# A 2-D Fourier transform ahead of a PReLU network: rows turned by ScalarE and GpSimd, and values split ahead of a butterfly

## The chip, the cores and the metric

One core of a Trainium2 chip. The metric is the device time of one execution in microseconds. TensorE multiplies into PSUM, VectorE, ScalarE and GpSimd do the rest; each of the five engines works through its own instructions in order and waits for the others by semaphores.

## The reference, cut to what matters

```
def _attn_ref(x):                       # x: 8 x 3072 x 256, float32
    X = np.fft.fft(x, axis=1)
    X = np.fft.fft(X, axis=2)
    return X.real.astype(np.float32)

def _moe_ref(x, w_in, w_out, alpha):    # x: 24576 x 256; 256 x 2048, 2048 x 256, 2048
    h = x @ w_in
    g = np.maximum(h, 0.0) + alpha * np.minimum(h, 0.0)
    return g @ w_out
```

The second takes the first's result, with its batches and rows put one behind the other.

## The kernel before, in words

**The steps.** The output is made in 26 blocks of columns, up to 512 wide. The eight batches b have three blocks each, the first and the last four. A block has 16 steps, one for each 128 of the 2048 hidden units, so there are 416 steps s = 16 g + f. The code calls a step's place within its batch the round r.

One step of TensorE holds six matmuls of `ffn1` for step s + 3 (`LEAD` = 3: two groups of three, each group into one PSUM bank of the pool `pq`, lines L665 to L667) and twelve of `ffn2` for step s (into four accumulator banks, L748; in the first block's steps up to f = 13 eight at L732). At the end of a block the accumulators are copied out, two by ScalarE (L762) and two by VectorE (L764), and stored.

**What lies between the two.** `pair(s + 3)` follows on the other engines. `sums` (VectorE, L683) makes `pf` from the first bank and the row `xbc`. Then for each half i of 0 and 1: `row` makes `d` = `pf` minus or plus the second bank (VectorE, L691) and `ad`, which is `d` times a scale, on ScalarE (L695), into the half's own PSUM bank. `split` takes `d` and `ad` of the step before: VectorE makes their maximum, which is the PReLU (L647; L644 for steps below `WHOLE` = 14), ScalarE rounds it to `hi` (L649), and GpSimd makes the rest `lo` = `d` - `hi` (L651). `st1` holds the values that have `d` and `ad` but aren't split yet, `st2` those that `ffn2` may use. With the read of `ad` in `split` the half's bank is free.

**The four banks.** The pool `pq` has four banks, handed out in the order of the program among those that have no more readers to come. The transforms of the next batch use the same banks. So `other_bank`, which `dft` calls for a bank, first splits the first half (i = 0) of whatever is under way.

**The transform.** While a batch is in its steps, the next one is folded along its rows by GpSimd and VectorE (`fold_piece`, up to round 36, in the first batch 50), into the tiles `ce`, `co`, `se` and `so` of 128x6x128. The scratch tiles of the fold have the tags `xev` and `xeg`, one buffer each. Then the even tiles go through `unit` (four times), and the odd ones through `turn_rows` and `mids` (rounds 44 and 46; 60 and 62 in the first batch) and, in rounds 0 and 3 of their own batch, `unit_odd`. The first batch has its own `turn_rows` in rounds 12 and 13, without `mids`, the second of them right behind `fold_128` (two small copies on GpSimd), and its `unit_odd` in rounds 16 and 19.

`turn_rows` takes the six planes of 128x128 of an odd tile in pairs: planes 3 to 5 times a tangent for each partition, plus planes 0 to 2, into the tile `a` (names `aco`, `aso`), and planes 0 to 2 times the negative tangent, plus planes 3 to 5, in place (`fco`, `fso`). These are six instructions of VectorE (L443). `mids` rounds the middle plane of both to `mh` (ScalarE, L479) and makes the rest `ml` (GpSimd, L480).

`unit_odd` issues the products `ca` and `sb` of the two (L501, L504), each into one bank, and then a butterfly of each: ScalarE copies half of the bank to `os` (L512), VectorE adds and subtracts it (`y`, L523, two instructions). VectorE puts the two results together (`yo`, L545, L547, in tiles with the tags `xev` and `xeg`), and `to_x` writes them as high and low part (ScalarE L575, GpSimd L576) to `X`, which `ffn1` reads.

The order of each engine's instructions is that of the program (`manual_schedule`); the round numbers place the work by hand:

```
            if q in (0, 3):
                unit_odd(b, ("co", "so")[q // 3])
...
                for nm, at in zip(("se", "ce", "co", "so"), (51, 52, 60, 62) if b == 0 else (37, 37, 44, 46)):
                    if r == at:
                        if nm[1] == "o":
                            turn_rows(b + 1, nm)
                        mids(b + 1, nm)
```

Of the kernel before, what the change touches and what calls it, by code (L numbers as in the profile page):

```python
# [9 lines left out]
F32 = mybir.dt.float32  # L10
# [6 lines left out]
ACTF = mybir.ActivationFunctionType  # L17
ALU = mybir.AluOpType

NB, N, D, DFF = 8, 3072, 256, 2048  # L20
P = 128
# [3 lines left out]
WM = 512  # L25
# [23 lines left out]
def _place(b, kind):  # L49

    return {"ee": 0, "eo": 385, "o": 769}[kind[1:]] + (b == 0 and kind[1:] != "ee")
# [82 lines left out]
def fft2_prelu_ffn(ctx: ExitStack, tc: tile.TileContext, t, outputs):  # L134
# [6 lines left out]
    foldp = ctx.enter_context(tc.tile_pool(name="foldp", bufs=1))  # L141
    small = ctx.enter_context(tc.tile_pool(name="small", bufs=1))
    work = ctx.enter_context(tc.tile_pool(name="work", bufs=2))
# [8 lines left out]
    V, S, G = nc.vector, nc.scalar, nc.gpsimd  # L152
# [3 lines left out]
    alpha, turns = consts[:, 0:KF], consts[:, KF:KF + 6]  # L156
    sg = small.tile([P, KF], F32, name="sg")
# [80 lines left out]
    def other_bank():  # L238

        for s, i in list(st1):  # L240
            if i == 0 and s >= WHOLE:
                split(s, i)
        return pq.tile([P, 512], F32, tag="pq", name="ps")
# [7 lines left out]
    WHOLE, KEPT = 14, 8  # L251
# [133 lines left out]
    def fold_sums(i):  # L385

        b, c, h = PIECES[i]
        r = buf["x", i].rearrange("p (j i) s d -> p i s j d", i=2)
        ps = accp.tile([P, 512], F32, tag=f"acc{(i + 1) // 2}", name="fold")
        for k in range(2):  # L390
            for n, (i_, s_) in enumerate(((0, 0), (0, 1), (1, 0), (1, 1))):
                nc.tensor.matmul(
                    out=ps[:, 256 * k:256 * k + 256], lhsT=ident[:, k * (i_ ^ s_)], rhs=r[:, i_, s_],
                    start=(n == 0), stop=(n == 3),
                )
        use("x", i)
        halves = ps.rearrange("p (k a j d) -> p k j a d", k=2, a=2, j=2)
        v = foldp.tile([P, 2, 2, 64], F32, tag="xeg", name="xeg")
        S.activation(out=v, in_=halves[:, :, 1], func=ACTF.Copy)
        return halves[:, :, 0], v  # L400
# [37 lines left out]
    def turn_rows(b, nm):  # L438

        v, a = fold[b, nm], fold[b, "a" + nm]  # L440
        for out, i, j in ((a, 1, 0), (v[:, 3:6], 0, 1)):
            for c in range(3):
                V.scalar_tensor_tensor(  # L443
                    out=out[:, c], in0=v[:, 3 * i + c], scalar=turns[:, 3 * j + c:3 * j + c + 1],
                    in1=v[:, 3 * j + c], op0=ALU.mult, op1=ALU.add,
                )

    def rows_384():

# [37 lines left out]
    def dft(kind, v, zr, m, mid=None, bank=None):  # L487

        ps = (bank or other_bank())[0:m]
        tab, at = TABS[kind]  # L490
        n = tab.shape[-1]
        even, odd = [(v[:, 0], tab[:, at])], [(v[:, 2], tab[:, at + 3])]
        if zr is not None:
            even.append((zr, tab[:, 4]))
        if mid is None:
            even.append((v[:, 1], tab[:, at + 1]))
            odd.append((v[:, 1], tab[:, at + 2]))
        else:
            (fh, fl), (th, tl) = mid, middle[kind]
            for i, (lhsT, rhs) in enumerate(((fh, th), (fh, tl), (fl, th))):  # L500
                nc.tensor.matmul(out=_pairs(ps[:, 0:2 * n]), lhsT=lhsT, rhs=_halves(rhs), start=(i == 0), stop=False)  # L501
        for o, terms in ((0, even), (n, odd)):
            for i, (lhsT, rhs) in enumerate(terms):
                nc.tensor.matmul(  # L504
                    out=ps[:, o:o + n], lhsT=lhsT, rhs=rhs, start=(mid is None and i == 0),
                    stop=(i == len(terms) - 1 and (o > 0 or mid is None)),
                )
        return ps, n, m

    def odd_sums(ps, n, m):  # L510
        os = foldp.tile([P, 193], F32, tag="os", name="os", bufs=2)[0:m, 0:n]
        S.activation(out=os, in_=ps[:, n:2 * n], func=ACTF.Copy)  # L512
        return ps, os, n, m

    def butterfly(ps, n, m, last=None):
        return both_sums(*odd_sums(ps, n, m), last=last)

    def both_sums(ps, os, n, m, pool=foldp, tag="y", last=None):
        wide, bufs = (WM, 1) if tag == "pf" else (WX, 2)
        last = last or n  # L520
        y = pool.tile([P, wide], F32, tag=tag, name="y", bufs=bufs)[0:m, 0:n + last]
        for i, (op, k) in enumerate(((ALU.subtract, n), (ALU.add, last)) if n == 193 else ((ALU.add, n), (ALU.subtract, n))):
            V.tensor_tensor(out=y[:, i * n:i * n + k], in0=ps[:, 0:k], in1=os[:, 0:k], op=op)  # L523
        return y
# [9 lines left out]
    def mid_of(nm, i):  # L534
        return [m[:, i * P:(i + 1) * P] for m in middle[nm]] if nm in middle else None

    def unit_odd(b, nm, whole=True):

        z = zres[:, 1 if nm == "co" else 2]
        ps = [  # L540
            dft("ca", fold[b, "a" + nm], z, P, mid_of(nm, 0)), dft("sb", fold[b, nm][:, 3:6], None, P, mid_of(nm, 1)),
        ]
        ya, yb = (butterfly(*v, last=192) for v in ps)
        y = [foldp.tile([P, 512], F32, tag="xe" + e, name="yo")[:, 0:385] for e in "vg"]
        V.tensor_tensor(out=y[0], in0=ya, in1=yb, op=ALU.add)  # L545
        for o, n, at in ((0, 192, 1), (192, 191, 194)):
            V.tensor_tensor(out=y[1][:, o:o + n], in0=ya[:, at:at + n], in1=yb[:, at:at + n], op=ALU.subtract)  # L547
        at = _place(b, nm)
        for o, v in ((0, y[0]), (385, y[1][:, 0:383])):
            if nm == "so":  # L550
                nc.sync.dma_start(out=xcd[b:b + 1, at + o:at + o + v.shape[-1]], in_=v[0:1])
            to_x(0 if nm == "co" else 2, at + o, v, G)

    def unit(b, kind, lo_engine):
        sums = unit_mm(b, kind, pq.tile([P, 512], F32, tag="pq", name="ps"))
        for s, i in list(st1):
            if i == 0:
                split(s, i)
        unit_store(b, kind, lo_engine, butterfly(*sums))
# [13 lines left out]
    def to_x(s, c, v, lo_engine):  # L573
        hi, lo = (X[:, s + i, X0 + c:X0 + c + v.shape[-1]] for i in range(2))
        S.activation(out=hi, in_=v, func=ACTF.Copy)  # L575
        lo_engine.tensor_tensor(out=lo, in0=v, in1=hi.bitcast(F32), op=ALU.subtract)  # L576
# [58 lines left out]

    st1, st2 = {}, {}

    def split(s, i):

        d, ad, f = st1.pop((s, i))  # L640
        w = d.shape[-1]
        if s < WHOLE:
            g = work.tile([P, WM], F32, tag=f"hi{i}", name="gw", bufs=3)[:, 0:w]
            V.scalar_tensor_tensor(out=g, in0=d, scalar=sg[:, f:f + 1], in1=ad, op0=ALU.mult, op1=ALU.max)  # L644
            st2[s, i] = g
            return
        V.scalar_tensor_tensor(out=d, in0=d, scalar=sg[:, f:f + 1], in1=ad, op0=ALU.mult, op1=ALU.max)  # L647
        hi = work.tile([P, WM], F32R, tag=f"hi{i}", name="hi", bufs=3)[:, 0:w]
        S.activation(out=hi, in_=d, func=ACTF.Copy)  # L649
        lo = work.tile([P, WM], F32R, tag=f"lo{i}", name="lo", bufs=3)[:, 0:w]  # L650
        G.tensor_tensor(out=lo, in0=d, in1=hi.bitcast(F32), op=ALU.subtract)  # L651
        st2[s, i] = hi, lo

    psum = {}

# [158 lines left out]
    sums = {0: fold_sums(0)}  # L814
# [67 lines left out]
    for b in range(NB):  # L882
# [3 lines left out]
        for r in range(len(mine) * KF):  # L886
            s = mine[0] * KF + r
            g, f = divmod(s, KF)
            step(s)
            if b == 0:  # L890
                if r == 3:
                    G.memset(X[:, :, X0 + SINGLE:X0 + SINGLE + 7].bitcast(F32), 0.0)  # L892
                    nc.sync.dma_start(out=er, in_=t["er"])
                if r == 9:
                    column_128_store("ceo", butterfly(*column_128_mm("ceo")))
                if r in (10, 11):
                    unit(0, ("ceo", "seo")[r - 10], G)
                if r in (12, 13):
                    if r == 13:
                        fold_128(0)  # L900
                    turn_rows(0, ("co", "so")[r - 12])
                if r == 25:
                    start.close()
                    late = ctx.enter_context(tc.tile_pool(name="late", bufs=1))
                if r in TABLE_STEPS:
                    parts_table(list(TABS)[TABLE_STEPS.index(r)])
# [3 lines left out]
            if q in (0, 3):  # L910
                unit_odd(b, ("co", "so")[q // 3])
# [85 lines left out]
```

## Time and profile before

| what | value |
| --- | --- |
| median of 3 runs | 1694.53 us (1693.9 to 1694.86) |
| profiled execution | 1695.3 us |
| its span, first to last instruction | 1693.5 us |
| mean granted clock of TensorE | 0.996 |
| TensorE busy | 1647.7 us, 97% |
| VectorE busy | 1533.3 us, 91% |
| GpSimd busy | 1295.1 us, 76% |
| ScalarE busy | 1112.9 us, 66% |

All times that are read from the trace count from the start of the span. In the rows PE is TensorE, PEld its loading of weights, DVE VectorE, ACT ScalarE, POOL GpSimd and SP the engine that issues most transfers. L443 is line 443 of the kernel. A matmul's end is modelled and reaches into the next one, so TensorE's pace is read from starts. A group of instructions says what it writes and reads by the names of the program's tiles (out<-in).

### The profile page before, as it was taken

To read this page: it belongs to the slowest core of one execution; us is meant where nothing else is said; L and a number is where in the kernel's file an instruction comes from. 1 tells how busy PE (TensorE), PEld (TensorE's weight loads), DVE (VectorE), ACT (ScalarE), POOL (GpSimd) and SP (SyncE) were. 2 spreads that over 40 slices of the span, in tenths; PEclk is the share of its full clock that TensorE was granted. 3 is DMA by queue.
4 is the path that set the end of the run, shared out by engine and by line. 5 is a ranking of instruction groups with operands and counts; after the bars stand their busy time and mean duration, and the time that the engine had idled before them with its cause. 6 is when DMAs were issued, how large, how long until landed. Compare 5 with 4: busy or idle time off the path is not lost.

```text
span 1693.5 us, 26291 instructions
## 1 busy us (share of the span) xinstructions
PE 1647.7 (97%) x8154; PEld 1460.6 (86%) x8154; DVE 1533.3 (91%) x2726; ACT 1112.9 (66%) x1998; POOL 1295.1 (76%) x1388
## 2 busy tenths in 40 slices
PE   8999999999999999999999999999999999999998
PEld 6678898888878888788888888888887888889998
DVE  7889999899899998999989998899989999899997
ACT  5856776666666666666666666666666666667675
POOL 2358996788868887689876998678886888766666
PEclk9999999999999999999999999999999999999999
DMA  6310110010100110001100011001010010000000
GB/s 236 130 62 6 57 68 20 7 62 22 55 26 14 62 38 32 26 19 57 63 7 32 38 45 57 25 8 64 26 50 26 19 45 31 1 31 24 25 20 20
DMA packets 25290, 69.94 MB, mean 41 GB/s; under 512 B 6174, under 2 KB 7486, under 8 KB 25150
## 3 DMA queue, kind: packets, MB, share of 16 engines
q1 hardware_dynamic: 24398, 67.80, 11.3%
q8 instruction: 65, 1.06, 0.3%
q14 instruction: 75, 0.61, 0.1%
q10 hardware_dynamic: 752, 0.45, 0.1%
HBM read 42.98 MB, written 25.25 MB: 40 GB/s over the span
## 4 chain that ended last, share of the span: by engine, by line
PE 82%; DVE 11%; issue 2%; POOL 2%; ACT 1%; DMA 1%; DVEq 0%; ACTq 0%; SPq 0%; POOLq 0%
PE acc L748 50%; PE pq L665 9%; PE pq L667 8%; PE pq L666 8%; DVE d L691 3%; PE ps L504 3%; DVE d L647 2%; DVE pf L683 2%; PE ps L501 1%; PE acc L732 1%; POOL lo L651 1%; DVE aco L443 1%; DVE aso L443 1%; ACT hi L649 1%; DVE fso L443 0%
## 5 line engine op out<-in xcount | busy, mean ns | idle before, releaser
L651 POOL TENSOR_TENSOR lo<-d,hi 128x512 fp32r<-128x512 f32 (+2 forms) x804 | 974.6, 1227 | 268.9 <-ACT hi L649 251.4
L649 ACT ACTIVATE hi<-d 128x512 fp32r<-128x512 f32 (+2 forms) x804 | 483.3, 601 | 394.0 <-DVE d L647 307.3
L647 DVE SCALAR_TENSOR_TENSOR d<-d,sg,pq 128x512 f32<-128x512 f32 (+2 forms) x804 | 563.8, 701 | 0.2 <-ACT pq L695 0.2
L695 ACT ACTIVATE pq<-d,sga 128x512 f32<-128x512 f32 (+2 forms) x804 | 527.3, 656 | 48.9 <-DVE d L691 47.5
L691 DVE TENSOR_TENSOR d<-pf,pq 128x512 f32<-128x512 f32 (+2 forms) x832 | 530.6, 639 | 12.4 <-POOL lo L651 4.1
L748 PE MATMUL acc<-hi,woh 128*128 128x512 f32 (+2 forms) x1608 | 455.2, 365 | 0.0
L748 PE MATMUL acc<-hi,wol 128*128 128x512 f32 (+2 forms) x1608 | 394.2, 365 | 0.0
L748 PE MATMUL acc<-lo,woh 128*128 128x512 f32 (+2 forms) x1608 | 393.0, 364 | 0.0
L683 DVE SCALAR_TENSOR_TENSOR pf<-xbc,w,pq 128x512 f32<-128x512 f32 (+2 forms) x416 | 297.8, 716 | 71.9 <-PE pq L667 65.0
L665 PE MATMUL pq<-X,wih 128*128 128x512 f32 (+2 forms) x832 | 317.2, 381 | 31.6 <-DVE d L647 28.0
L748 PEld LDWEIGHTS acc<-hi,woh 128*128 128x128 f32 x1608 | 298.5, 189 | 31.0
L748 PEld LDWEIGHTS acc<-hi,wol 128*128 128x128 f32 x1608 | 295.9, 189 | 32.1 <-DVE o L764 0.3
L748 PEld LDWEIGHTS acc<-lo,woh 128*128 128x128 f32 x1608 | 295.4, 189 | 30.9
L666 PE MATMUL pq<-X,wih 128*128 128x512 f32 (+2 forms) x832 | 302.4, 364 | 2.7 <-POOL X L892 2.5
L667 PE MATMUL pq<-X,wil 128*128 128x512 f32 (+2 forms) x832 | 302.5, 364 | 0.0
L665 PEld LDWEIGHTS pq<-X,wih 128*128 128x128 f32 x832 | 157.3, 189 | 71.6 <-DVE d L647 25.1
L666 PEld LDWEIGHTS pq<-X,wih 128*128 128x128 f32 x832 | 157.6, 189 | 16.5 <-POOL X L892 2.8
L667 PEld LDWEIGHTS pq<-X,wil 128*128 128x128 f32 x832 | 157.5, 189 | 15.6 <-DVE wil L337 0.2
L523 DVE TENSOR_TENSOR y<-ps,os 128x193 f32<-128x193 f32 (+3 forms) x132 | 40.5, 353 | 54.2 <-ACT os L512 54.1
L383 POOL TENSOR_TENSOR raw<-raw 128x512 f32<-128x512 f32 (+2 forms) x84 | 69.3, 825 | 0.0
L289 POOL TENSOR_TENSOR w<-we,wm 128x512 int32<-128x512 int32 x16 | 20.3, 1270 | 52.3 <-DVE wm L280 47.9
L576 POOL TENSOR_TENSOR X<-yo,X 128x385 fp32r<-128x385 f32 (+1 forms) x32 | 29.1, 932 | 28.6 <-ACT X L575 28.6
(155 smaller groups left out, 1027.2 us busy)
## 6 DMA issues: line engine op xcount, KB each, us to landing
raw<-in_xh SPq DMA_DIRECT2D x46, 512.0 KB
out<-o SPq DMA_DIRECT2D x36, 512.0 KB
raw<-in_w SPq DMA_DIRECT2D x15, 512.0 KB
xbc<-xcd SPq DMA_DIRECT2D x18, 256.0 KB
out<-o SPq DMA_DIRECT2D x10, 386.0 KB
out<-o SPq DMA_DIRECT2D x6, 384.0 KB
before<-in_xh SPq DMA_DIRECT2D x2, 512.0 KB
xbc<-xcd SPq DMA_DIRECT2D x5, 193.0 KB
```

The source lines that it names most:

```text
L383: yield size, lambda o=o, i0=i0, i1=i1, op=op: e.tensor_tensor(out=o, in0=i0, in1=i1, op=op)
L504: nc.tensor.matmul(out=ps[:, o:o + n], lhsT=lhsT, rhs=rhs, start=(mid is None and i == 0), stop=(i == len(terms) - 1 and (o > 0 or mid is ...
L647: V.scalar_tensor_tensor(out=d, in0=d, scalar=sg[:, f:f + 1], in1=ad, op0=ALU.mult, op1=ALU.max)
L649: S.activation(out=hi, in_=d, func=ACTF.Copy)
L651: G.tensor_tensor(out=lo, in0=d, in1=hi.bitcast(F32), op=ALU.subtract)
L665: nc.tensor.matmul(out=out, lhsT=wih[:, f, q], rhs=xh, start=True, stop=False)
L666: nc.tensor.matmul(out=out, lhsT=wih[:, f, q], rhs=xl, start=False, stop=False)
L667: nc.tensor.matmul(out=out, lhsT=wil[:, f, q], rhs=xh, start=False, stop=True)
L683: V.scalar_tensor_tensor(out=_pairs(pf), in0=_halves(xbc[g]), scalar=w128[:, f:f + 1], in1=_pairs(ps[0]), op0=ALU.mult, op1=ALU.add,)
L691: V.tensor_tensor(out=d, in0=pf, in1=ps[1], op=ALU.add if i else ALU.subtract)
L695: S.activation(out=ad, in_=d, func=ACTF.Copy, scale=sga[:, f:f + 1])
L748: nc.tensor.matmul(out=out, lhsT=wt[:, f, o * P:(o + 1) * P], rhs=rhs, start=(f == 0 and n[o] == 0), stop=(f == KF - 1 and n[o] == 2),)
```

## The change

`turn_rows` no longer uses VectorE: for each of the two results ScalarE multiplies three planes by their tangents into a scratch tile (tag `xev` for the first, `xeg` for the second), and GpSimd adds three planes in one instruction. All six multiplications are issued ahead of the two additions. `split` is cut into `split_sum` (VectorE's maximum) and `split_parts` (`hi` and `lo`). `unit_odd` calls `split_sum` for all values under way as soon as both products are issued, which leaves the second half, since `other_bank` has split the first; then ScalarE's copies `os` of both products are issued, then `split_parts`, then the additions of both butterflies. Elsewhere `split` does what it did.

```
     def turn_rows(b, nm):
 
         v, a = fold[b, nm], fold[b, "a" + nm]
-        for out, i, j in ((a, 1, 0), (v[:, 3:6], 0, 1)):
+        made = []
+        for e, i in (("v", 1), ("g", 0)):
+            part = foldp.tile([P, 512], F32, tag="xe" + e, name="part")[:, 0:384].rearrange("p (c d) -> p c d", c=3)
             for c in range(3):
-                V.scalar_tensor_tensor(
-                    out=out[:, c], in0=v[:, 3 * i + c], scalar=turns[:, 3 * j + c:3 * j + c + 1],
-                    in1=v[:, 3 * j + c], op0=ALU.mult, op1=ALU.add,
-                )
+                at = 3 * (1 - i) + c
+                S.activation(out=part[:, c], in_=v[:, 3 * i + c], func=ACTF.Copy, scale=turns[:, at:at + 1])
+            made.append(part)
+        G.tensor_tensor(out=a, in0=v[:, 0:3], in1=made[0], op=ALU.add)
+        G.tensor_tensor(out=v[:, 3:6], in0=v[:, 3:6], in1=made[1], op=ALU.add)
...
-        ya, yb = (butterfly(*v, last=192) for v in ps)
+        parted = [(s, i, *split_sum(s, i)) for s, i in list(st1)]
+        sums = [odd_sums(*v) for v in ps]
+        for v in parted:
+            split_parts(*v)
+        ya, yb = (both_sums(*v, last=192) for v in sums)
...
-    def split(s, i):
+    def split_sum(s, i):
 
         d, ad, f = st1.pop((s, i))
+        g = d
+        if s < WHOLE:
+            g = work.tile([P, WM], F32, tag=f"hi{i}", name="gw", bufs=3)[:, 0:d.shape[-1]]
+            st2[s, i] = g
+        V.scalar_tensor_tensor(out=g, in0=d, scalar=sg[:, f:f + 1], in1=ad, op0=ALU.mult, op1=ALU.max)
+        return (g,)
+
+    def split_parts(s, i, d):
         w = d.shape[-1]
...
+    def split(s, i):
+        g = split_sum(s, i)
+        if s >= WHOLE:
+            split_parts(s, i, *g)
```

## Rows read from the trace of the kernel before

**Rows 1.** The page: busy time, share of the span, instructions of each engine.

```profile
PE 1647.7 (97%) x8154; PEld 1460.6 (86%) x8154; DVE 1533.3 (91%) x2726; ACT 1112.9 (66%) x1998; POOL 1295.1 (76%) x1388
```

**Rows 2.** Busy time by stretch: from:to, length, engines, granted clock, DMA.

```profile
100.00:150.00 50.00, 43.79 (x235) 38.42 (x234) 42.14 (x90) 29.64 (x65) 34.24 (x41) 1.00 0.06 21
...
276.00:300.00 24.00, 19.98 (x94) 16.96 (x94) 21.56 (x41) 14.40 (x28) 14.73 (x15) 0.93 0.09 34
300.00:478.00 178.00, 178.00 (x836) 156.16 (x835) 163.39 (x269) 116.87 (x196) 147.58 (x153) 1.00 0.10 35
478.00:504.00 26.00, 23.24 (x107) 19.11 (x106) 24.73 (x46) 15.41 (x30) 16.69 (x17) 1.00 0.10 41
...
678.00:704.00 26.00, 23.24 (x108) 19.08 (x107) 24.75 (x45) 16.32 (x31) 16.53 (x16) 1.00 0.10 41
1480.00:1530.00 50.00, 47.58 (x265) 43.89 (x264) 45.90 (x93) 32.12 (x65) 31.89 (x34) 1.00 0.07 26
```

**Rows 3.** The chain that ended last, 470 to 506 us: start, length, what.

```profile
474.94 0.76 DVE pf L683
...
486.50 0.66 DVE d L647
...
493.46 0.45 PE pq L665
```

**Rows 4.** Timeline, 474 to 497 us: start, length, engine; in brackets idle before, releaser.

```profile
474.08 0.38 PE L665 MATMUL pq<-X,wih 128*128 128x512 f32 x1
...
477.18 2.57 POOL L651 TENSOR_TENSOR lo<-d,hi 128x512 fp32r<-128x512 f32 x2 [1.50 <-ACT hi L649]
...
477.97 0.38 PE L665 MATMUL pq<-X,wih 128*128 128x512 f32 x1
...
478.12 2.04 DVE L443 SCALAR_TENSOR_TENSOR aco<-fco,consts 128x128 f32<-128x128 f32 x3
...
478.30 0.69 ACT L695 ACTIVATE pq<-d,sga 128x512 f32<-128x512 f32 x1
...
481.12 0.75 DVE L683 SCALAR_TENSOR_TENSOR pf<-xbc,w,pq 128x512 f32<-128x512 f32 x1
...
482.58 0.48 PE L665 MATMUL pq<-X,wih 128*128 128x512 f32 x1 [0.56 <-DVE d L647]
...
496.78 0.33 PE L501 MATMUL ps<-mh 128*128 128x386 f32 x1
```

**Rows 5.** Timeline behind the products of the third batch's first odd transform.

```profile
499.60 0.54 ACT L512 ACTIVATE os<-ps 128x193 f32<-128x193 f32 x2
...
499.95 1.15 DVE L523 TENSOR_TENSOR y<-ps,os 128x193 f32<-128x193 f32 x4 [1.00 <-ACT os L512]
...
500.72 0.45 PE L665 MATMUL pq<-X,wih 128*128 128x512 f32 x1 [0.51 <-DVE y L523]
```

**Rows 6.** Groups by line: count | busy us, mean ns | idle before, releaser.

```profile
L443 DVE SCALAR_TENSOR_TENSOR aco<-fco,consts 128x128 f32<-128x128 f32 x24 | 15.9, 713 | 0.0
...
L545 DVE TENSOR_TENSOR yo<-y 128x385 f32<-128x385 f32 x16 | 9.0, 564 | 0.6
...
L479 ACT ACTIVATE mh<-aco 128x128 fp32r<-128x128 f32 x7 | 2.2, 312 | 6.5 <-DVE aco L443 6.5
...
L576 POOL TENSOR_TENSOR X<-y,X 128x384 fp32r<-128x384 f32 x16 | 15.8, 988 | 4.4 <-ACT X L575 3.6
```

**Rows 7.** Line L651: duration in ns, least/median/most, first and last start.

```profile
L651 POOL TENSOR_TENSOR lo<-d,hi x804: 990/1281/1743, 105.2 to 1685.6; 128x512 fp32r<-128x512 f32 x116, 128x386 fp32r<-128x386 f32 x26, 128x384 fp32r<-128x384 f32 x19
```

**Rows 8.** Timeline of the first two batches: three waits.

```profile
114.60 0.88 DVE L443 SCALAR_TENSOR_TENSOR aso<-fso,consts 128x128 f32<-128x128 f32 x3 [1.43 <-POOL fso L420]
...
131.32 0.40 PE L665 MATMUL pq<-X,wih 128*128 128x384 f32 x1 [0.70 <-DVE d L647]
...
290.12 0.48 PE L665 MATMUL pq<-X,wih 128*128 128x512 f32 x1 [1.96 <-DVE d L647]
```

More of the change, by code (lines that the diff above doesn't have):

```diff
@@ L636, in fft2_prelu_ffn @@
     st1, st2 = {}, {}
-    def split(s, i):
+    def split_sum(s, i):
         d, ad, f = st1.pop((s, i))
-        w = d.shape[-1]
[L642 to L647, printed above, removed]
+        g = d
[5 more added lines that the diff above has]
+    def split_parts(s, i, d):
+        w = d.shape[-1]
         hi = work.tile([P, WM], F32R, tag=f"hi{i}", name="hi", bufs=3)[:, 0:w]
```

## The prediction, made before the result was known

> **What bounds the kernel now.** I read the page first: TensorE is busy 97% of the span, VectorE 91%, GpSimd 76%, ScalarE 66% [rows 1]. So the question is not which engine is fullest, but where TensorE stands still and for whom. The table by stretches answers the first half. From 300 to 478 us, one whole stretch between two batches, TensorE is busy 178.00 of 178 us: nothing can be won there. In the 26 us around a change of batch it is busy 23.24; the rows of the second and third such change are the same to 0.01 us, and there are five of this kind. The first batch (100 to 150 us), the step to the second (276 to 300 us) and the step to the last (1480 to 1530 us) lack 6.2, 4.0 and 2.4 us [rows 2]. The chain of work that ended last says for whom: from 474.94 to 493.46 us not one matmul is on it, only VectorE with short stretches of issue [rows 3]. The change of batch is bound by VectorE, all else by TensorE.
>
> The timeline shows how [rows 4]. A step of 18 matmuls takes 477.97 - 474.08 = 3.89 us. Then `turn_rows` puts six instructions on VectorE: it starts them at 478.12, and the next step's `pf` follows at 481.12 instead of 474.94 + 3.89 = 478.83. The PSUM banks of `ffn1` come free with VectorE's `split` (the line L647), so the next step's first matmul starts at 482.58, 4.61 us after the one before. From 477.97 to the first product of `unit_odd` at 496.78 there are four steps, 18.81 us where 4 x 3.89 = 15.56 would do: 3.25 us lost for the two turns of a batch. The idle times that the rows name understate this: the gap of 0.56 us cost 4.61 - 3.89 = 0.72 us, and the second matmul behind a gap starts about 0.1 us late as well. I count 0.26 us on top of each gap.
>
> **What the turns cost after the change.** The change takes 6 x 16 = 96 instructions from VectorE (the costliest quarter of them means 713 ns [rows 6]) and adds 6 x 16 multiplications on ScalarE and 2 x 16 additions of 128x384 on GpSimd. For ScalarE the nearest row is the 128x128 `mh`, 312 ns; for GpSimd the 128x384 subtraction of `to_x`, 988 ns [rows 6]. No row shows these very operations. From below, the six could overlap at their ends and take less than 6 x 0.31; from above, a GpSimd pass could cost what the dearest `lo` did, 1743 ns [rows 7], which I keep for the range.
>
> In total that is some 30 us of ScalarE and 32 us of GpSimd, both with room. What matters is the queue. Behind the turn ScalarE has `mids`, which since the change waits for GpSimd's sums; ScalarE works in order, so the `hi` and `ad` of the next step are held too, and VectorE's `split` waits for `ad`. Take the first turn in numbers of [rows 4, 6]. ScalarE is done with `ad` at 478.30 + 0.69 = 478.99. Three multiplications: 479.93; six: 480.86. GpSimd has finished both `lo` at 477.18 + 2.57 = 479.75, so its sums run 479.93 to 480.92 and on to 481.91. The second `mh` ends at 482.22, then one `hi` and one `ad` of at most 0.69 us each: 483.60. Without a delay VectorE comes to the `split` that needs this `ad` one `pf` after 474.94 + 2 x 3.89 = 482.72, at 482.72 + 0.75 = 483.47. ScalarE is 0.13 us late, and the bank that this `split` frees is needed only by the matmuls at 477.97 + 2 x 3.89 = 485.75, so TensorE doesn't see it. But no slack is left: whatever the sums take beyond this goes through.
>
> The second turn is followed by the copies of the finished accumulators on ScalarE, held by the same wait; the matmul that needs the second of them then comes about 0.1 us too early. After that TensorE has the products of `unit_odd`, in which ScalarE catches up. I leave 0.15 us of the 3.25.
>
> GpSimd's other work is not late by this: `lo` of the held step is needed two steps later, and the fold of the next batch has ended before (round 36, the turns are at 44 and 46). The two buffers that the products take are those of the fold and of `yo`, both done with by then. No DMA is added, and no queue's order changes but that of the row that `unit_odd` sends, which waits for the same `yo`.
>
> **What the split made early brings.** In `unit_odd` only the first half of the values under way is split today; the second half's `split` stands behind the butterflies and the next `pf`. The second `ffn1` group then takes a bank of the products and waits 0.51 us for the butterfly [rows 5]; with 0.26 on top that is 0.77 us. After the change the second half's `split` stands ahead of the butterflies. Its `ad` comes before `os` on ScalarE, and VectorE idles 1.00 us there for `os` [rows 5], more than one `split` takes (0.66 us [rows 3]). It costs nothing, and the wait goes. In the first batch the same pattern costs more: 0.70 us at 131.32 [rows 8], the first of three such gaps.
>
> **A rule against it.** GpSimd needs 988 ns for 384 columns where VectorE's `yo` of 385 columns, also from SBUF, needs 564: 1.75 times as much [rows 6]. The Trainium skill ("GPSIMD Engine Reference", section 4.1, Engine selection) says to add tiles on VectorE, as GpSimd is about twice as slow with two inputs; the trace agrees in direction. By its factor a sum would take an estimated 1.13 us, the hold at each of 14 turns would be 0.28 us longer, and the result 3.9 us later, near 1665 us; the sum below keeps to the row.
>
> **The sum.** Five ordinary changes of batch: 3.25 + 0.77 - 0.15 = 3.87 us each, 19.3 us.
> The second batch: gaps of 4.0 us [rows 2] at four places, 1.0 on top, and a granted clock of 0.93 over 24 us, 1.7 us: the clock sinks behind the gap of 1.96 us [rows 8]. 6.7 us in all. Its steps are narrower on TensorE while VectorE's are not, so I leave 0.9 us: 5.8 won.
> The last batch: 2.4 us of gaps [rows 2] at six places, 1.6 on top, and by the starts of its matmuls 0.5 at short stalls without a gap: 4.5, of which I leave 0.8: 3.7.
> The first batch: 5.6 us of the 6.2 [rows 2] (0.6 belong to a `unit`, which isn't changed), at eight places, 1.9 on top: 7.5. Its second turn waits today for GpSimd's copy `fold_128`, 1.43 us [rows 8]; after the change ScalarE waits for that same copy, with its own queue behind it. I leave 2.1: 5.4 won.
> Together 19.3 + 5.8 + 3.7 + 5.4 = 34.2 us. The profiled execution took 1695.3 us, so 1661.1; the median of the runs is 0.8 us below it. I predict 1661 us. If nothing is left over, 20.1 + 6.7 + 4.5 + 7.5 = 38.8 us go: 1656.5.
>
> **Rivals.**
> *ScalarE becomes the new wait.* For it speaks that the working above ends without slack. If a sum takes 1743 ns, the second `mh` ends 2 x 0.755 = 1.5 us later, and at 14 turns (those of the first batch have no `mids`) that is 21 us: 1682; half of it: 1672. Against it: no 128x384 row of GpSimd here is near that price. Chance 0.15.
> *The early split doesn't free the bank in time.* Then 5 x 0.77, some 2.5 in the first batch and 1.2 in the last are not won, 7.6 us: 1669. Against it is VectorE's idle time ahead of the butterflies. Chance 0.07.
> *Nothing is won.* The hold on ScalarE just replaces that on VectorE. It needs 34.2 / 14 = 2.4 us more per turn, sums of 2.2 us each: 1692 to 1698. Chance 0.05.
> *Slower.* The same place, GpSimd's two sums ahead of `mids`, past that point: at 2.6 us each the hold grows by 2 x 1.61 = 3.2 us, 45 us in all against 34 won: 1706. VectorE's first product of a turn does take several times as long as its last beside GpSimd (its three need 2.04 us at 478.12 [rows 4]), so such prices exist; but with the turn gone, what VectorE does meanwhile (`pf`, `d`, `split`) reads one input from PSUM, as it does beside every `lo`. Chance 0.03.
> The forecast has what is left, 0.70, with a range of its own of 1656 to 1668.
>
> **The numbers.** A measurement of this kernel tells 0.2% (3.4 us) from no change. The three cases ahead of "nothing is won" are all faster: 0.70 + 0.15 + 0.07 = 0.92; the same 0.05; slower 0.03. The range that leaves out no more than 2 in 10 goes from 1655 (all stalls gone, by the median) to 1677, which takes in the early split's failure and the milder two thirds of ScalarE's.
>
> **What would show it.** Right: around 478 to 504 us VectorE has no work of a turn, TensorE's waits for `split` there are gone, the clock stays at 1.00 near 290 us, and ScalarE's `mh` waits for GpSimd about 1 us. The bank step: no wait for `y` behind `unit_odd`. Wrong: GpSimd's sums above 1.2 us each, VectorE idle ahead of `split` for `ad`, or a wait of TensorE for ScalarE's copies of the accumulators at the end of a batch.

## The result, and the profile after

The changed kernel takes 1675.0 us (median; 1674.0 to 1675.8) against 1694.2 of the kernel before: a ratio of 0.9887, interval 0.987 to 0.9904, 19.2 us faster. That lies in the range, but the predicted time was 1661, with 34 us won: the change brought little more than half of it. (The result and the experiments are medians of several executions; a profile is of one of them, up to 3 us longer or shorter.)

The page of the changed kernel, its line of busy times and the chain's shares by engine:

```profile
PE 1642.9 (98%) x8154; PEld 1462.0 (87%) x8154; DVE 1512.8 (90%) x2630; ACT 1133.8 (68%) x2094; POOL 1328.4 (79%) x1420
...
PE 88%; DVE 6%; POOL 2%; issue 2%; ACT 1%; DVEq 0%; POOLq 0%; ACTq 0%
```

Against [rows 1] VectorE has its 96 instructions less and 20.5 us less work, where [rows 6] put the costliest quarter of them alone at 15.9 us; so some of its work has become longer. The table by stretches (as in [rows 2]; the changes of batch now come earlier):

```profile
270.00:304.00 34.00, 32.15 (x162) 27.92 (x161) 30.92 (x51) 25.36 (x55) 26.37 (x26) 1.00 0.06 24
304.00:472.00 168.00, 167.80 (x789) 147.42 (x788) 155.02 (x252) 110.62 (x187) 142.41 (x148) 1.00 0.10 37
472.00:500.50 28.50, 27.78 (x131) 23.75 (x130) 25.51 (x40) 21.88 (x47) 23.33 (x23) 1.00 0.10 38
```

Between the batches TensorE is as busy as before. Around an ordinary change of batch it now stands still for 28.50 - 27.78 = 0.72 us, where the same 28.5 us of the kernel before (478 to 506.5) had 2.76. Near 290 us the clock stays at 1.00.

The timeline of the changed kernel around the first turn of the third batch, which answers to [rows 4]:

```profile
472.29 0.69 ACT L709 ACTIVATE pq<-d,sga 128x512 f32<-128x512 f32 x1
...
472.92 1.85 ACT L446 ACTIVATE part<-fco,consts 128x128 f32<-128x128 f32 x6
...
473.97 1.01 POOL L448 TENSOR_TENSOR aco<-fco,part 128x384 f32<-128x384 f32 x1 [0.26 <-ACT part L446]
...
474.94 1.00 POOL L449 TENSOR_TENSOR fco<-fco,part 128x384 f32<-128x384 f32 x1
...
475.97 0.31 ACT L482 ACTIVATE mh<-fco 128x128 fp32r<-128x128 f32 x1 [0.65 <-POOL fco L449]
...
476.71 0.67 ACT L709 ACTIVATE pq<-d,sga 128x512 f32<-128x512 f32 x1
...
477.41 0.75 DVE L652 SCALAR_TENSOR_TENSOR d<-d,sg,pq 128x512 f32<-128x512 f32 x1
```

The turn went as worked out: the six multiplications take 1.85 us, each sum 1.0, the second `mh` ends 3.30 us after the last `ad` of the step before (predicted 3.23), and the held `ad` ends at 477.38, 0.03 us ahead of the `split` that needs it. TensorE doesn't wait.

Behind `unit_odd` it does. First the kernel before, for comparison (timeline, 497 to 503 us), then the changed kernel's timeline that answers to [rows 5]:

```profile
497.26 3.79 POOL L651 TENSOR_TENSOR lo<-d,hi 128x512 fp32r<-128x512 f32 x3 [1.86 <-ACT hi L649]
...
501.13 0.56 DVE L545 TENSOR_TENSOR yo<-y 128x385 f32<-128x385 f32 x1
501.61 0.62 DVE L547 TENSOR_TENSOR yo<-y 128x192 f32<-128x192 f32 x2
```

```profile
485.83 7.79 POOL L660 TENSOR_TENSOR lo<-d,hi 128x512 fp32r<-128x512 f32 x6 [1.03 <-ACT hi L658]
...
489.91 0.75 DVE L652 SCALAR_TENSOR_TENSOR d<-d,sg,pq 128x512 f32<-128x512 f32 x1 [0.16 <-ACT pq L709]
...
490.73 1.16 DVE L526 TENSOR_TENSOR y<-ps,os 128x193 f32<-128x193 f32 x4
...
491.92 0.57 DVE L552 TENSOR_TENSOR yo<-y 128x385 f32<-128x385 f32 x1
...
492.41 2.51 DVE L554 TENSOR_TENSOR yo<-y 128x192 f32<-128x192 f32 x2
...
493.59 1.12 POOL L583 TENSOR_TENSOR X<-yo,X 128x385 fp32r<-128x385 f32 x1
...
494.84 0.75 DVE L697 SCALAR_TENSOR_TENSOR pf<-xbc,w,pq 128x512 f32<-128x512 f32 x1
...
498.60 0.48 PE L679 MATMUL pq<-X,wih 128*128 128x512 f32 x1 [0.28 <-DVE d L652]
...
499.94 0.45 PE L679 MATMUL pq<-X,wih 128*128 128x512 f32 x1 [0.43 <-DVE d L652]
```

The early `split` at 489.91 does lie in VectorE's idle time, and the wait for `y` is gone. But the two short `yo` instructions take 2.51 us; in the kernel before they took 0.62, behind GpSimd's last `lo`, which had ended at 501.05. Now they start while GpSimd is still in its row of six `lo`, which ends at 493.62, and then in `to_x`. VectorE comes to the next `pf` late, and two steps on TensorE waits for `split` twice, about 1.2 us by the starts of its matmuls, where 0.77 was to go.

### The profile page after: what moved, and what is told of

Read it like the earlier page. It is cut to its first block, busy times and chain, and to the rows that moved or that the text cites. A ratio compares the mean times of both kernels' runs of the same rounds, so it can differ in the third digit from the quotient of the medians.

```text
span 1673.9 us, 26326 instructions
## 1 busy us (share of the span) xinstructions
PE 1642.9 (98%) x8154; PEld 1462.0 (87%) x8154; DVE 1512.8 (90%) x2630; ACT 1133.8 (68%) x2094; POOL 1328.4 (79%) x1420
## 4 chain that ended last, share of the span: by engine, by line
PE 88%; DVE 6%; POOL 2%; issue 2%; ACT 1%; DVEq 0%; POOLq 0%; ACTq 0%
PE acc L762 54%; PE pq L679 9%; PE pq L680 9%; PE pq L681 9%; PE ps L507 3%; DVE d L705 2%; PE ps L504 2%; PE acc L746 1%; DVE pf L697 1%; DVE d L652 1%; POOL lo L660 1%; PE fold L392 0%; PE ps L320 0%; DVE we L276 0%; DVE wm L280 0%
## 5 line engine op out<-in xcount | busy, mean ns | idle before, releaser
L652 DVE SCALAR_TENSOR_TENSOR d<-d,sg,pq 128x512 f32<-128x512 f32 (+2 forms) x804 | 565.5, 703 | 11.1 <-ACT pq L709 11.1
L776 ACT ACTIVATE o<-acc 128x512 f32<-128x512 f32 (+2 forms) x52 | 26.4, 559 | 25.3 <-PE acc L762 25.3
```

## The experiments

The explanation to test (theory A): the early `split` gives GpSimd a `lo` just when VectorE makes `yo` from two tiles in SBUF, and VectorE's instruction can't run beside it. The rival (B): the order of VectorE's own work is to blame, in which the two `d` of the next step now stand next to each other. Diffs are against the changed kernel unless another is named.

**The turns alone.** `unit_odd` is that of the kernel before:

```
-        parted = [(s, i, *split_sum(s, i)) for s, i in list(st1)]
-        sums = [odd_sums(*v) for v in ps]
-        for v in parted:
-            split_parts(*v)
-        ya, yb = (both_sums(*v, last=192) for v in sums)
+        ya, yb = (butterfly(*v, last=192) for v in ps)
```

> Only the turns go to ScalarE and GpSimd; unit_odd is that of the kernel before. In the changed kernel the turns' stalls fell from 3.25 us a batch to 0.26, but behind unit_odd a wait of 0.77 us became one of 1.22 us two steps later. Theory A (GpSimd's lo, made earlier, runs while VectorE makes yo from two tiles in SBUF, and holds it): yo is near 0.56 and 0.35 us again, the wait for y of about 0.5 us is back, the wait two steps later is gone: 1675 - 5 x 0.45 - about 2 in the first, second and last batch = 1671 us. Rival (the early split is worth its 0.77 us, as predicted, and something else was lost): 1675 + 7.6 = 1683 us.

1670.2 us, a ratio of 0.9855 (0.9841 to 0.9869): 24.0 us won by the turns. The early `split`, added to them, cost 4.8. The mean times of `yo` are 588 and 350 ns, and waits for `y` are back, though of 0.3 us at most: as theory A has it.

**The early split alone.** `turn_rows` is that of the kernel before:

```
     def turn_rows(b, nm):
...
+        for out, i, j in ((a, 1, 0), (v[:, 3:6], 0, 1)):
+            for c in range(3):
+                V.scalar_tensor_tensor(
...
```

> Only the split of unit_odd is made early; the turns stay on VectorE. Theory A: lo runs beside yo here too, so yo takes 1.2 us or more in most of the 16 places, and the 0.77 us won are paid back: 1694 to 1698 us. Rival (as the prediction had it, the early split is free): 1694 - 7.6 = 1687 us. Added to the first kernel of this set it also says whether the two parts add up: the sum of both gains should be the 19.2 us of the whole change within 2 us.

1694.5 us, 0.9995 (0.9986 to 1.0004): nothing won. The groups of `yo` (columns as in [rows 6]) in this kernel and, below, in the changed one:

```profile
L549 DVE TENSOR_TENSOR yo<-y 128x385 f32<-128x385 f32 x16 | 23.4, 1460 | 0.6
L551 DVE TENSOR_TENSOR yo<-y 128x192 f32<-128x192 f32 (+1 forms) x32 | 11.3, 392 | 0.0
```

```profile
L554 DVE TENSOR_TENSOR yo<-y 128x192 f32<-128x192 f32 (+1 forms) x32 | 21.2, 701 | 0.0
L552 DVE TENSOR_TENSOR yo<-y 128x385 f32<-128x385 f32 x16 | 18.6, 1165 | 0.5
```

The 564 ns of [rows 6] became 1460 and 1165, and the short forms' 350 became 392 and 701. The parts don't add up: 24.0 - 0.3 = 23.7 us won apart and 19.2 together, outside the 2 us that the expectation allowed. The turns delay GpSimd's `lo`, so that in the whole change more of them run beside `yo`: in the third batch the first `yo` group takes 3.00 us from its start to its end in the changed kernel, 2.11 with the early split alone, and 1.10 in the kernel before.

The traced execution of this kernel (1696.5 us, the longest of eleven) also has a stall at another place, in the first batch (timeline, 190 to 204 us):

```profile
192.63 5.36 DVE L383 TENSOR_TENSOR xev<-raw 128x512 f32<-128x512 f32 x1
...
196.15 1.28 POOL L383 TENSOR_TENSOR xeg<-raw 128x512 f32<-128x512 f32 x1
...
199.82 0.69 PE L676 MATMUL pq<-X,wih 128*128 128x384 f32 x1 [4.73 <-DVE d L649]
```

A VectorE instruction of the fold with two inputs in SBUF took 5.36 us where 0.69 is usual: GpSimd had instructions without a pause from before its start to 197.43, and it ended 0.56 us behind the last of them. How often this happens in the other ten executions isn't known, so the total of 1694.5 is not a clean price of the early split. The five ordinary changes of batch are clear of it. From the first product of a batch TensorE needs this long to the start of the 224th matmul behind it, in each of the five within 0.02 us: 47.77 us in the kernel before, 47.73 with the early split alone, 47.58 with the turns alone, 48.42 in the changed kernel. The 0.8 us won at the bank are lost again, 0.4 at a time, two steps behind each of the two `unit_odd` of a batch.

**The parts behind to_x.** GpSimd gets the early half's `lo` only when `yo` is done:

```
         sums = [odd_sums(*v) for v in ps]
-        for v in parted:
-            split_parts(*v)
         ya, yb = (both_sums(*v, last=192) for v in sums)
...
             to_x(0 if nm == "co" else 2, at + o, v, G)
+        for v in parted:
+            split_parts(*v)
```

> The changed kernel, but hi and lo of the half split early are issued behind to_x, so that GpSimd has less to do while VectorE makes yo; VectorE's own order is that of the changed kernel. Theory A: yo falls from up to 3.1 us to below 1.7 us for the three, the wait two steps behind unit_odd (1.2 us a batch) goes: 1675 - 12 = 1663 us. Rival B (the wait comes from VectorE's changed order, the two d now standing next to each other, and not from yo): the wait stays, 1675 us within 2.

1665.6 us, 0.9828 (0.9814 to 0.9841). VectorE's order is untouched, and `yo` is short again:

```profile
L552 DVE TENSOR_TENSOR yo<-y 128x192 f32<-128x192 f32 (+1 forms) x32 | 9.9, 349 | 0.0
L550 DVE TENSOR_TENSOR yo<-y 128x385 f32<-128x385 f32 x16 | 9.5, 593 | 0.5
```

That speaks for A and against B; 9.4 of the 12 us expected came. Most of the rest is the same hold at another place: in six batches the `lo` that was put off now runs beside the fold's first instruction, which reads two tiles in SBUF (timeline, 486 to 512 us; 0.69 us alone):

```profile
505.84 1.28 POOL L660 TENSOR_TENSOR lo<-d,hi 128x512 fp32r<-128x512 f32 x1
...
505.97 1.71 DVE L383 TENSOR_TENSOR xev<-raw 128x512 f32<-128x512 f32 x1
```

Two steps later TensorE loses about 0.5 us in each of the six.

**The second operand in PSUM.** The same `lo` at the same place in every engine's order, but `yo` reads one of its inputs from the second butterfly's bank:

```
-        ya, yb = (both_sums(*v, last=192) for v in sums)
+        ya = both_sums(*sums[0], last=192)
+        pb, ob, n, _ = sums[1]
+        V.tensor_tensor(out=pb[:, n:n + 192], in0=pb[:, 0:192], in1=ob[:, 0:192], op=ALU.add)
+        V.tensor_tensor(out=pb[:, 0:n], in0=pb[:, 0:n], in1=ob, op=ALU.subtract)
+        yb = pb[:, 0:385]
```

> The changed kernel, but the second butterfly's result stays in its PSUM bank, so that each of VectorE's yo instructions reads one input from SBUF and one from PSUM; every engine's order and GpSimd's lo are those of the changed kernel. Theory A: yo takes about 0.56 and 0.35 us in all 16 places although lo runs beside it, and the wait two steps later goes: 1675 - 13 = 1662 us. Rival B (VectorE's changed order): 1675 us within 2, or later, since the bank is held for 1.3 us more.

1661.6 us, 0.9806 (0.979 to 0.9822). The timeline of this kernel at the same place as above, and its groups of `yo`:

```profile
483.91 3.76 POOL L664 TENSOR_TENSOR lo<-d,hi 128x512 fp32r<-128x512 f32 x3
...
486.41 0.56 DVE L556 TENSOR_TENSOR yo<-y,ps 128x385 f32<-128x385 f32 x1
...
486.88 0.61 DVE L558 TENSOR_TENSOR yo<-y,ps 128x192 f32<-128x192 f32 x2
```

```profile
L558 DVE TENSOR_TENSOR yo<-y,ps 128x192 f32<-128x192 f32 (+1 forms) x32 | 9.8, 346 | 0.0
L556 DVE TENSOR_TENSOR yo<-y,ps 128x385 f32<-128x385 f32 x16 | 8.9, 557 | 0.5
```

GpSimd is in its `lo` until 487.67, all through the `yo` at 486.41 and 486.88, and they take their ordinary time. In the whole trace 45 of the 48 `yo` start beside a GpSimd instruction, and none takes more than 0.56 us (385 columns) or 0.35 us (192). This decides for A: with one input in PSUM the hold is gone, at the same order and the same amount of work. Why two inputs in SBUF are held isn't shown by the runs. Early `split` and PSUM operand together are worth 1670.2 - 1661.6 = 8.6 us over the turns alone; the prediction had 7.6 for the early `split`. The PSUM operand without the early `split` wasn't run; with the turns alone `yo` takes 19.3 us in all and here 18.7, so little of the 8.6 can be due to `yo` itself being shorter.

**The sums made twice.** From the kernel with the operand in PSUM, to price the hold on ScalarE:

```
-        G.tensor_tensor(out=a, in0=v[:, 0:3], in1=made[0], op=ALU.add)
+        for _ in range(2):
+            G.tensor_tensor(out=a, in0=v[:, 0:3], in1=made[0], op=ALU.add)
+        G.tensor_tensor(out=made[0], in0=v[:, 3:6], in1=made[1], op=ALU.add)
         G.tensor_tensor(out=v[:, 3:6], in0=v[:, 3:6], in1=made[1], op=ALU.add)
```

> The kernel with the second butterfly in PSUM (1661.6 us), but GpSimd makes each of the two sums of a turn twice, the first time into the same place or into scratch: two more passes of 1.0 us between ScalarE's products and mids, nothing else. It prices the hold on ScalarE. The prediction's rule (no slack is left, whatever the sums take beyond goes through): 14 turns x 2.0 = 28 us, 1690 us. Rival (TensorE still has the distance between the split and the matmul that takes its bank, 0.8 to 1.5 us, ahead of it in the first turn, and in the second the held accumulator copies reach it at once): about 1 us and 2 us, 7 batches x 3 = 21 us, 1682 us. If the hold has much more room than either, below 1670 us.

1701.5 us: 1.0043 (1.0029 to 1.0056) of the kernel before, and 39.9 us more than without. Both expectations were too low. The timeline of this kernel, ScalarE, VectorE and TensorE behind the doubled sums, and one stretch:

```profile
481.05 2.10 POOL L449 TENSOR_TENSOR aco<-fco,part 128x384 f32<-128x384 f32 x2 [0.26 <-ACT part L446]
...
485.34 0.31 ACT L484 ACTIVATE mh<-fco 128x128 fp32r<-128x128 f32 x1 [1.85 <-POOL fco L451]
...
486.79 0.75 DVE L658 SCALAR_TENSOR_TENSOR d<-d,sg,pq 128x512 f32<-128x512 f32 x1 [2.25 <-ACT pq L715]
```

```profile
496.40 1.28 PE L768 MATMUL acc<-hi,woh 128*128 128x512 f32 x2 [2.57 <-ACT o L782]
```

```profile
486.00:500.00 14.00, 10.27 (x37) 7.70 (x36) 9.84 (x16) 10.85 (x24) 12.61 (x14) 0.85 0.17 68
```

By the starts of its matmuls the first turn costs TensorE 1.6 us more than without the doubling, where the rival had 1, and the second 2.8, where it had 2. By the second turn ScalarE has not caught up: it is busy without a pause from 485.34 to the second turn's products at 490.24, so the hold reaches the accumulators' copies with what was left of the first: a gap of 2.57 us. Behind that gap the granted clock falls to its lower level, 1.2 GHz, 0.85 over the 14 us: the third batch's matmuls run at half their pace until 502.7, which costs another 2.8 us. The clock does not fall behind every such gap: in the third to the seventh batch of this execution there are five of 2.57 us, and it fell behind the first two. Together with falls in the first two batches the lower clock took some 7 us here.

**The turns a round earlier.** From the kernel with the operand in PSUM:

```
-                for nm, at in zip(("se", "ce", "co", "so"), (51, 52, 60, 62) if b == 0 else (37, 37, 44, 46)):
+                for nm, at in zip(("se", "ce", "co", "so"), (51, 52, 59, 61) if b == 0 else (37, 37, 43, 45)):
```

> The kernel with the second butterfly in PSUM, its turns in rounds 43 and 45 (59 and 61) instead of 44 and 46 (60 and 62), so that a whole step lies between the hold on ScalarE and its copies of the accumulators. If the stalls of 0.25 us in five batches, 1.1 us at the second and 1.3 us at the last come from those copies standing behind the hold, they go: 1661.6 - 3.7 = 1658 us. Rival (the step itself is too narrow for the hold, wherever it stands): 1661 to 1662 us.

1659.7 us, 0.9794 (0.978 to 0.9807): 1.9 us less than without, half of the 3.7, and the intervals of the two overlap. The cause was right all the same. Among TensorE's waits in the kernel with the operand in PSUM (total, times, longest) stands

```profile
PE acc L766 <- ACT o L780: 1.4, 2, 0.7
```

and in this kernel no such wait is left. Matmul by matmul, 0.24 us went at each of the five ordinary changes of batch and 1.3 us at the last. At the second batch a wait for `split` takes its place (0.27 and 0.55 us), so the narrow steps there are too short for the hold wherever it stands.

**fold_128 earlier as well.** From the last one:

```
-                    if r == 13:
+                    if r == 12:
                         fold_128(0)
```

> The kernel before this one in the set, and in the first batch GpSimd's small copies (fold_128) are issued in round 12, ahead of the first turn, instead of round 13 behind two lo. ScalarE's wait for them (1.49 us) goes, and with it TensorE's 0.2 and 1.1 us at 117 and 119 us of the changed kernel: 1658 - 1.6 = 1656 us. Rival (those two stalls come from the sums and the weights' work on ScalarE and not from the copies): 1658 us within 1.

1658.2 us, 0.9787 (0.9774 to 0.9801): 1.5 us less, though the intervals overlap here too. The traces agree: the two gaps of 0.2 and 1.1 us became one of 0.48, and ScalarE's wait for the copies (1.5 us in the changed kernel) is gone. This is the fastest version of the study, 16.8 us ahead of the changed kernel and 36 ahead of the kernel before.

## Why the prediction was right in its direction and wrong in its size

*The range.* That the time lies in it is luck. The range reached up to 1677 us for two rivals, a bank that comes free too late and a slow sum ahead of `mids`. Neither of them is what cost the time; what did stood in no term of the prediction.

*Where TensorE loses time.* Right: all that was won came from the first batch and the changes of batch; the stretches between stayed as they were. (That the rows of two changes of batch are the same to 0.01 us holds for TensorE's 23.24 alone; ScalarE's differ by 0.9 us [rows 2].) Us won by place, from the starts of the same matmuls in the traces (100, 270, 470 and 1470 us of the kernel before part the places; the fastest version is that with `fold_128` earlier):

| place | predicted | turns alone | changed kernel | fastest version |
| --- | --- | --- | --- | --- |
| first batch | 5.4 | 2.2 | 2.4 | 5.3 |
| second batch | 5.8 | 4.3 | 3.5 | 5.0 |
| five ordinary batches | 19.3 | 15.9 | 11.8 | 21.8 |
| last batch | 3.7 | 1.8 | 1.8 | 4.0 |

With the hold on `yo` gone and two smaller repairs, what the prediction expected did come.

*The turns.* Right in mechanism and nearly in size: 24.0 us measured, 34.2 - 7.6 = 26.6 in the sum without the early `split`. An ordinary batch's two turns cost TensorE 0.23 us now, after 3.24, by the starts of its matmuls; 0.15 had been left. The rest is missing where the steps are narrow: at the second batch and the last the copies of the accumulators stand behind the hold for 0.7 us each, at a place where I had foreseen 0.1. The prices were good: six multiplications in 1.85 us where 1.87 was taken, a sum 1009 ns where 988 was taken, and so nearer to the row than to the 1.13 us estimated from the factor in the Trainium skill ("GPSIMD Engine Reference", section 4.1, Engine selection). Two of the signs named for "wrong" did show, at a small price: VectorE is idle ahead of `split` for `ad` 27 times, 11.1 us in all, and TensorE waits twice for copies of the accumulators.

*The early split.* Here the prediction failed, in the sentences "It costs nothing, and the wait goes" and "GpSimd's other work is not late by this". The cover that it named, VectorE's idle microsecond, was there. It asked whether GpSimd would be late, and not whom GpSimd would now run beside: the moved step issues a `lo` too, the turns' sums push GpSimd's row back, and the row met `yo`. Counted at 7.6 us won, it lost 4.8; 8.6 are to be had once `yo` reads one input from PSUM. The difference of 12.4 us between 7.6 won and 4.8 lost is most of the 15 us between the 34.2 forecast and the 19.2 won, and the turns' 2.6 are the rest.

*The trace of before showed it.* The prediction even named a sign, the first three instructions of a turn at 2.04 us beside GpSimd [rows 4], and set it aside because the turn was to go; three such instructions take 0.88 us at 114.60 [rows 8], where GpSimd is all but idle. (Of the three at 478.12 it is not the first that takes several times as long as the last, but the second: 0.49, 1.36 and 0.34 us.) `yo` has the same two inputs in SBUF. In the kernel before GpSimd is idle at the start of 15 of the 16 groups of `yo`, in five of them since less than 0.1 us: they were short by luck of the order. The sign also says what the turns' old price was made of: from its first instruction to the next `pf` a turn took VectorE 3.0 us beside `lo`, and 1.58 at 114.60. Nearly half of it was this hold; a turn left on VectorE but clear of GpSimd was not tried.

*The rivals.* The early split didn't fail in the way that the second rival named: the bank came free in time. That ScalarE's hold leaves no slack was right, and its price was put too low: with sums that take twice as long, 2.0 to 2.1 us, the kernel is slower than before (1701.5 us), where the prediction put the point of no gain at 2.2 us. It forgot that two turns are only two steps apart, so that the second inherits what is left of the first, and that a longer gap can bring the clock down.

*The clock.* With the gap of 1.96 us gone, the dip near 290 us went, as expected; the longest gap there is now 0.72 us.

## What to carry to other kernels

When a step is moved, ask of each instruction that it releases on the other engines what runs there at its new time, not only whether it is late. An instruction of VectorE with two inputs in SBUF, of fp32 as here, should not meet a row of GpSimd's instructions; give it one operand in PSUM, or put GpSimd's work behind it. Where an in-order engine is made to wait for a slower one, count what is held behind the wait up to the next wait of that kind, not each wait by itself.

## What the runs showed of the hardware

In the changed kernel 28 of the 48 `yo` started beside an instruction of GpSimd. All but one ended 0.42 us (385 columns) or 0.21 us (192 columns) after that instruction's own end, whether they had waited 0.15 or 1.2 us, as if no element got through until GpSimd's instruction was over. The same holds for the turns in the kernel before: at 880.48 us one of 128 columns starts 0.10 us after a `lo` and ends 0.15 us behind its end, 1.36 us for what otherwise takes 0.34.

In a row of GpSimd's instructions VectorE mostly gets in at the first boundary, but not always. The one exception among the 28, at 125.90 us, let a second `lo` pass, and the fold's instruction of the kernel with the early split alone was held through six boundaries, 5.36 us.

GpSimd pays too: the six `lo` that began while a `yo` with both inputs in SBUF was at work took 1.59 to 1.60 us where 1.28 is usual. The Trainium skill ("GPSIMD Engine Reference", section 8, Key points) says that GpSimd shares its SBUF interfaces with VectorE and that instructions with two SBUF inputs contend; the traces agree, and the sixteen `yo` groups with one input in PSUM, 1.08 us each from start to end beside the same `lo`, show the other side of it.
